# Where the second matmul's slots stand around the units of the first, in a convolution and two-layer kernel on one core

## Chip, cores and metric

One core of a Trainium2 chip. The metric is the device time of one execution in microseconds; the kernel before took 684.85 us in the median of five runs (684.1 to 686.18).

## The reference

`x` has the shape (8, 4096, 192), in float32. Each of 8 heads of 24 channels is convolved causally along the sequence with 7 taps, which are the softmax of the head's row of `weight`. The result, taken as 32768 rows of 192, goes through two matrices with a leaky ReLU between them.

```python
w = softmax(weight)                                   # (8, 7)
y[b, s, h*24+g] = sum_k w[h, k] * x_pad[b, s+k, h*24+g]   # 6 zero rows ahead
h = y.reshape(32768, 192) @ w_in                      # (192, 2048)
out = np.maximum(0.01 * h, h) @ w_out                 # (2048, 192)
```

## The kernel before

**Tiles.** Channels lie on partitions. Two batches are worked on at a time: partitions 0 to 63 hold 64 channels of the one (`e = 0`), 64 to 127 those of the other (`e = 1`), and the 192 channels are three such chunks (`NCH`). A block is 512 positions of such a pair of batches, and there are 32 blocks. The first three are cut in halves of 256: `groups` 0 to 5 are half blocks, group 6 on are full blocks.

**The way of a block.** GpSimd's queue loads x and casts it to bf16 (`load_x`, L83). SyncE's queue transposes it by DMA (`transpose_x`, L98). VectorE convolves it, seven instructions for each chunk (`conv_jobs`, L205 and L211), into `yt`. TensorE multiplies by `w_in` in units (`mm1`, L466) into one of two PSUM tiles `ph`, and ScalarE evacuates each with the leaky ReLU into `g` (L473). TensorE multiplies `g` by `w_out` in slots, and the result is evacuated and stored by SyncE's queue.

**Units and slots.** A unit of `mm1` yields 128 x 1024 values of g: 24 matmuls make two units of a half block, 12 of 512 columns two of a full block (in groups up to 6; behind that, tiles of 64*64 double the number). A unit needs one of the two `ph` tiles, so it waits for the activation of the unit before the last. Up to group 6 the second matmul is done by `mm2_row_slot`: one slot is two matmuls of 192 columns (L492), one on each half of TensorE's rows, for one pair of output tiles of 128 rows. Sixteen slots are a round; between the two rounds of a pair the halves change places, and an instruction of ScalarE, the seal (L527, later the evacuation L603), keeps the second round behind the first. After a pair's second round its first tile is evacuated, at the next seal the second, and then the store is issued (L609). From group 7 on `mm2_slot` does the second matmul with the operands exchanged (L555), and VectorE evacuates with a transpose (L577).

**The order.** It is written out by hand (the schedule is manual): each engine does its instructions in program order. A group is cut into steps, four for a half block and eight for a full one. A step is two units, and then a number of slots that `plan` gives, which belong to g of earlier groups:

```python
    plan = {
        0: [0] * 4,
        NSW - 2: [16, 8, 8, 16],
        NSW - 1: [8, 8, 16, 16],
        NSW: [16, 8, 8, 16, 8, 8, 16, 16],
    }
```

`NSW` is 6. Groups 1 to 3 have 16 slots in each step, and later groups a number for each of eight steps. Loads (`load_x`) and transposes (`transpose_x`) of later blocks are issued at fixed steps, after the slots. In half blocks VectorE's jobs for the next group come after the slots too.

**The start.** The first half block does not wait for the usual way: SyncE loads it in float32 (L125), it is cast (L138), and TensorE transposes it (`transpose_first`, L157 for the first half block with `q == 0`, L166 for two others) into PSUM tiles `ptr`, one of 128 positions each for `q == 0`. ScalarE evacuates the first and VectorE the second (`evac_first`, L177), and the convolution of the first groups runs on TensorE with diagonal matrices (`pe_conv_jobs`, L236). Junk matmuls (`warm`, L332) fill TensorE's time before.

Of the kernel before, what the change touches and what calls it, by code (L numbers as in the profile page):

```python
# [10 lines left out]
FP32 = mybir.dt.float32  # L11
BF16 = mybir.dt.bfloat16
# [3 lines left out]
def kernel(  # L16
# [8 lines left out]
    nc = tc.nc  # L25
# [11 lines left out]
    NCH = D // CH  # L37
# [3 lines left out]
    HS = SUB // 2  # L41
# [63 lines left out]
    def new_xt(rp):  # L105
# [7 lines left out]
    x_half = {  # L113
        q: const_pool.tile([128, NCH, HS, 2, CH], BF16, name=f"x_half{q}") for q in (0, 3)
    }
# [27 lines left out]
    ptr = {}  # L143

    def transpose_first(q):
        n = HS if q == 0 else 1
        ts = [
            psum_o.tile(
                [128, HS // n, NCH, 128], BF16 if q else FP32, name=f"ptr{i}", tag="po"
            )  # L150
            for i in range(n)
        ]
        for s in range(HS):
            t = ts[s * n // HS]
            for c in range(NCH):
                if q == 0:
                    nc.tensor.matmul(  # L157
                        out=t[:, 0, c, :],
                        lhsT=x_half[q][:, c, s, :, :].rearrange("p e k -> p (e k)"),
                        rhs=ident,  # L160
                        start=True,
                        stop=True,
                    )
                    continue
                for e in range(2):
                    nc.tensor.transpose(  # L166
                        out=t[e * CH : (e + 1) * CH, s, c, :],
                        in_=x_rows[q][:, e, s, c * CH : (c + 1) * CH],
                        identity=ident,
                    )  # L170
        ptr[q] = [t[:, s] for t in ts for s in range(HS // n)]
# [104 lines left out]
    for sign, off in ((1, 0), (-1, GRP - 1)):  # L276
        nc.gpsimd.affine_select(
            out=sel, in_=sel, compare_op=mybir.AluOpType.is_ge, fill=0.0,
# [31 lines left out]
    ident = const_pool.tile([128, 128], BF16)  # L310
# [3 lines left out]
    for rows in (0, 128):  # L314
# [6 lines left out]
        out=w_out.rearrange("p (c i) d -> p c i d", i=RUN),  # L321
        in_=moe_w_out.rearrange("(c p i) d -> p c i d", p=128, i=RUN),
# [123 lines left out]
    NSW = 2 * NHALF  # L446
# [7 lines left out]
    def mm1(grp, u, M):  # L454
        blk, t0, T = grp
        y = yt[blk]
        nf = ST // T
        ph = psum_h.tile([128, 2, ST], FP32, name="ph", tag="ph")
        chunks = range(NCH) if blk or t0 else FIRST
        for n in range(nf * NCH):  # L460
            i, c = n // NCH, chunks[n % NCH]
            f = nf * u + i
            for e in range(2):
                ps = slice(e * CH, (e + 1) * CH)
                for m in range(0, 128, M):
                    nc.tensor.matmul(  # L466
                        out=ph[m : m + M, e, i * T : (i + 1) * T],
                        lhsT=w_in_of(f, e, c, m, m + M),
                        rhs=y[ps, c, t0 : t0 + T],
                        start=(c == chunks[0]),  # L470
                        stop=(c == chunks[-1]),
                    )
        act = nc.scalar.activation(  # L473
            out=g[blk][:, nf * u : nf * (u + 1), :, t0 : t0 + T],
            in_=ph.rearrange("p e (i t) -> p i e t", i=nf),
            func=mybir.ActivationFunctionType.Prelu, alpha=0.01,
        )
        return act
# [21 lines left out]
    def mm2_row_slot(q):  # L500

        p, fc = divmod(q, 2 * NFC)
        rnd, fc = divmod(fc, NFC)
        pair = (2 * p, 2 * p + 1)
        first, last = fc == 0, fc == NFC - 1
        if first and rnd == 0:
            for n in pair:
                po[n] = psum_o.tile([128, D], FP32, name="po", tag="po")  # L510
        for rt in range(2):
            ins = mm2_one(
                rt, pair[rt ^ rnd], fc, first and rnd == 0, last and rnd == 1
            )
            if first and rnd == 1:
                sync(ins, seal, "both row tiles have left these banks")
        if last and rnd == 0:
            seal_round(p, ins)
        if last and rnd == 1:
            evac_o(pair[0])  # L520
# [14 lines left out]
    def mm2_slot(q):  # L535

        nonlocal seal
        gi, fc = divmod(q, NR * NFC)
        rnd, fc = divmod(fc, NFC)
        first, last = fc == 0, fc == NFC - 1
        if first:
            for r in ((1, 0), (2,), ())[rnd]:
                acc2[gi, r] = psum_o.tile([128, ST], FP32, name="acc2", tag="po")
        for rt in range(2):
            r = (rnd + rt) % NR
            fresh = (rnd, rt) in ((0, 0), (0, 1), (1, 1))  # L550
            done = (rnd, rt) in ((1, 0), (2, 0), (2, 1))
            b, t0, T = groups[gi]
            ps = slice(rt * CH, (rt + 1) * CH)
            for e in range(2):
                ins = nc.tensor.matmul(  # L555
                    out=acc2[gi, r][e * CH : (e + 1) * CH, 0:T],
                    lhsT=w_out_of(ps, fc, r),
                    rhs=g[b][ps, fc, e, t0 : t0 + T],
                    start=first and fresh,
                    stop=last and done,  # L560
                )
                if first and not fresh:
                    sync(ins, seal, "the other row tile has left this bank")
        if last and rnd < 2:
            seal = nc.scalar.copy(out=junk, in_=junk)  # L565
            sync(seal, ins, "between the rounds")
        if last and rnd > 0:
            for r in ((), (1,), (0, 2))[rnd]:
                evac_t(gi, r)
# [26 lines left out]
    def evac_o(n):  # L596
# [21 lines left out]
        NSW - 1: [8, 8, 16, 16],  # L618
        NSW: [16, 8, 8, 16, 8, 8, 16, 16],
    }  # L620
    slot = 0
    for i, grp in enumerate(groups):
        blk, t0, T = grp
        steps = T // 64
        if t0 == 0:
            g[blk] = g_pool.tile([128, NFC, 2, ST], BF16, name="g", tag="g")
        quota = plan.get(i, [16] * 4 if T == HT else [5, 5, 6, 5, 5, 6, 8, 8])

        if i == 0:
            ahead = []  # L630
        else:
            ahead = conv_jobs(groups[i + 1]) if i + 1 < len(groups) else []
        per = -(-len(ahead) // steps)
        for j in range(steps):
            for u in range(2 * j, 2 * j + 2):
                mm1(grp, u, 128 if i <= NSW else CH)
                if i == 0 and u == 0:
                    conv_1 = conv_jobs(groups[1], (1,))
                    for job in conv_1[:3]:
                        job()  # L640
                    spread_down(1)
                    spread_up(1)
                    for job in conv_1[3:]:
                        job()
                    pe_0, evac_0 = pe_conv_jobs(groups[1], 0)
                    pe_2, evac_2 = pe_conv_jobs(groups[1], 2, cross=True)
                if i == 0 and u in CUTS:
                    cut = slice(*CUTS[u])
                    run(pe_0[cut], pe_2[cut])
                if i == 0 and u == 5:  # L650
                    evac_0(nc.vector.tensor_scalar_mul)
                    evac_2(nc.vector.tensor_scalar_mul, nc.vector.tensor_scalar_mul)
                if i == 0 and u == 6:
                    transpose_first(2)
            jobs = ahead[per * j : per * (j + 1)]
            if T == ST:


                jobs = ahead[len(ahead) * j // steps : len(ahead) * (j + 1) // steps]
                for job in jobs:  # L660
                    job()
                jobs = []
            for _ in range(quota[j]):
                if i <= NSW:
                    mm2_row_slot(slot)
                else:
                    mm2_slot(slot)
                slot += 1
            if i == 0 and j == 3:
                evac_first(2, nc.vector.tensor_copy, nc.vector.tensor_copy)  # L670
            if i == 2 and j == 1:
                transpose_x(2)
            for job in jobs:
                job()
            if i == 0 and j == 3:
                transpose_half(3)

            last_half = t0 + T == ST
            if i == NSW and j == steps - 1:
                evac_o(LAST - 1)  # L680
                slot = NSW * NR * NFC
            if j == steps // 4 and last_half:
                load_x(blk + 3)
            if j == steps // 2 and last_half and blk > 0:
                transpose_x(blk + 2)
# [35 lines left out]
```

## Time and profile before

| | us |
|---|---|
| median of five runs | 684.85 |
| runs | 684.1, 684.27, 684.85, 685.35, 686.18 |
| the profiled execution, its own time | 686.18 |
| its span, first to last instruction | 684.3 |
| TensorE busy with matmuls in the span | 679.4 |
| ScalarE busy | 522.1 |
| VectorE busy | 483.1 |
| GpSimd busy | 145.5 |

The page of the profile gives for each engine the time in which an instruction was under way. For TensorE that is from a matmul's start to its modelled end, and matmuls overlap each other. A row of the timeline merges instructions of one line: start, time from the first start to the last end, engine, line, operation, operands, form and number, and in brackets the idle time before it with what ended it. The list of waits counts only time in which an engine had nothing under way. The groups stand at these times in the trace: group 1 begins at about 20 us, group 4 at 52.4, group 5 at 61.9, group 6 at 71.3 and group 7 at 90.1.

### The profile page before, as it was taken

How to read it: one execution, taken by the hardware profiler on the slowest of the kernel's cores; microseconds unless marked ns; L12 is line 12 of the kernel's file. 1: busy time of each engine (PE TensorE's matmuls, PEld its weight loads, DVE VectorE, ACT ScalarE, POOL GpSimd, SP SyncE). 2: the span in 40 equal slices, each digit the busy share in tenths (PEclk: the TensorE clock that was granted, in tenths of full speed). 3: DMA queues.
4: the chain of work that ended last, by engine and by line, in shares of the span. 5: the costliest groups of instructions: out<-in, count | busy, mean ns of one | idle time of the engine just before them, and what ended most of it. 6: DMA issues, size and time to landing. Idle time of an engine off the chain costs nothing.

```text
span 684.3 us, 27253 instructions
## 1 busy us (share of the span) xinstructions
PE 679.4 (99%) x12514; PEld 457.6 (67%) x12514; DVE 483.1 (71%) x827; ACT 522.1 (76%) x617; POOL 145.5 (21%) x204
## 2 busy tenths in 40 slices
PE   9999999999999999999999999999999999999998
PEld 6999766666666666666666666666666666666667
DVE  6979667667687667786667786676876676876612
ACT  6889987777877778777787777777777778777781
POOL 7722250222102222012222022222022220000000
PEclk9999999999999999999999999999999999999999
DMA  9966794579566577586676576596675684333123
GB/s 154 92 88 79 98 98 60 66 70 94 79 87 78 57 79 92 75 90 74 57 89 85 81 85 71 59 94 83 82 79 64 72 94 72 71 54 35 35 48 93
DMA packets 212786, 53.27 MB, mean 78 GB/s; under 512 B 207168, under 2 KB 212288, under 8 KB 212672
## 3 DMA queue, kind: packets, MB, share of 16 engines
q1 hardware_dynamic: 113920, 37.57, 33.5%
q0 software_dynamic: 98736, 13.97, 29.9%
q8 instruction: 97, 1.59, 0.9%
q14 instruction: 17, 0.14, 0.1%
q10 hardware_dynamic: 16, 0.00, 0.0%
HBM read 28.31 MB, written 25.17 MB: 78 GB/s over the span
## 4 chain that ended last, share of the span: by engine, by line
PE 97%; ACT 2%; DMA 0%; DVE 0%; issue 0%; SPq 0%
PE ph L466 48%; PE acc L555 42%; PE po L492 6%; ACT g L473 2%; PE acc L236 1%; DMA x_nat<-in_x_dram 0%; PE ptr L157 0%; DVE xt L177 0%; PE ptr L166 0%; SPq L125 0%; ACT x_half L138 0%; DVE o_sb L603 0%
## 5 line engine op out<-in xcount | busy, mean ns | idle before, releaser
L473 ACT ACTIVATE g<-ph 128x1024 bf16<-128x1024 f32 x512 | 496.3, 1021 | 138.5 <-PE ph L466 137.9
L211 DVE SCALAR_TENSOR_TENSOR yt<-xt,wk,yt 128x512 bf16<-128x512 bf16 (+1 forms) x600 | 380.9, 713 | 0.2
L466 PE MATMUL ph<-yt,w_in 64*64 64x512 bf16 (+2 forms) x6048 | 377.6, 366 | 0.5 <-ACT g L473 0.2
L555 PE MATMUL acc<-g,w_out 64*64 64x512 bf16 x5376 | 328.2, 376 | 0.0
L466 PEld LDWEIGHTS <-w_in 64*64 64x64 bf16 (+1 forms) x6048 | 234.4, 130 | 101.3 <-issue 2.5
L555 PEld LDWEIGHTS <-w_out 64*64 64x64 bf16 x5376 | 172.4, 118 | 114.6
L83 POOL DMA_DIRECT2D x_bf<-in_x_dram x180 | 133.8, 776 | 416.0 <-DMA xt<-x_bf 294.3
L577 DVE STREAM_TRANSPOSE o_t<-acc 128x512 f32<-128x512 f32 x84 | 70.6, 884 | 175.5 <-PE acc L555 175.5
L492 PE MATMUL po<-w_out,g 64*128 64x192 bf16 (+1 forms) x896 | 48.0, 243 | 0.0
L492 PEld LDWEIGHTS <-g 64*128 64x128 bf16 (+1 forms) x896 | 44.5, 95 | 1.6 <-issue 0.4
L205 DVE TENSOR_SCALAR yt<-xt,wk 128x512 bf16<-128x512 bf16 (+1 forms) x100 | 28.1, 343 | 10.3 <-DMA xt<-x_bf 10.3
L565 ACT COPY junk<-junk 128x1 f32<-128x1 f32 x56 | 10.7, 191 | 4.3 <-ACT g L473 0.3
L603 ACT COPY o_sb<-po 128x192 f32<-128x192 f32 x24 | 7.6, 320 | 0.8
L603 DVE COPY o_sb<-po 128x192 f32<-128x192 f32 x8 | 2.8, 357 | 6.8 <-PE po L492 6.8
L236 PE MATMUL acc<-xt,diag 64*64 64x256 bf16 x140 | 7.0, 328 | 0.2 <-DVE xt L177 0.2
L236 PEld LDWEIGHTS <-diag 64*64 64x64 bf16 x140 | 5.3, 131 | 2.1 <-DVE xt L177 0.8
L332 PE MATMUL warm<-const-bfloat16-1.0 128*128 128x512 bf16 (+1 forms) x12 | 4.2, 490 | 0.8 <-PEq L705 0.8
L132 POOL DMA_DIRECT2D x_half<-in_x_dram x6 | 4.3, 764 | 0.0
L396 ACT ACTIVATE diag<-ident,whm 128x64 bf16<-128x64 bf16 x14 | 3.6, 336 | 0.2 <-DVE whm L382 0.2
L332 PEld LDWEIGHTS <-const-bfloat16-1.0 128*128 128x128 bf16 x12 | 1.4, 131 | 2.5 <-issue 2.5
L128 POOL DMA_DIRECT2D x_rows<-in_x_dram x4 | 2.9, 742 | 0.0
L424 ACT ACTIVATE yt<-acc,rsum 128x256 bf16<-128x256 f32 (+1 forms) x3 | 1.4, 473 | 1.6 <-PE acc L236 1.6
(46 smaller groups left out, 24.2 us busy)
## 6 DMA issues: line engine op xcount, KB each, us to landing
out_dram<-o_t SPq DMA_DIRECT2D x112, 192.0 KB, 3.9
x_bf<-in_x_dram POOLq DMA_DIRECT2D x180, 64.0 KB, 3.1
out_dram<-o_sb SPq DMA_DIRECT2D x12, 192.0 KB, 2.6
xt<-x_bf SPq DMA_TRANSPOSE x90, 3.3
w_out<-in_moe_w_out_dram POOLq DMA_DIRECT2D x1, 768.0 KB, 9.1
out_dram<-o_sb SPq DMA_DIRECT2D x8, 96.0 KB, 1.7
w_in<-in_moe_w_in_dram POOLq DMA_DIRECT2D x2, 256.0 KB, 4.7
x_nat<-in_x_dram SPq DMA_DIRECT2D x2, 192.0 KB, 2.9
```

The costliest lines, as they stand in the source:

```text
L83: nc.gpsimd.dma_start(out=t[:, c, :, e, :], in_=src[2 * rp + e, :, :, c * CH : (c + 1) * CH],)
L205: lambda s=src, d=dst, c=c: nc.vector.tensor_scalar_mul(d, s, wk[:, c, 0:1])
L211: lambda s=src, d=dst, c=c, k=k: nc.vector.scalar_tensor_tensor(out=d, in0=s, scalar=wk[:, c, k : k + 1], in1=d, op0=mybir.AluOpType.mult, ...
L236: lambda k=k, p=p, a=a, ps=ps, to=to, acc=accs[e * apart]: nc.tensor.matmul(out=acc[to, :T], lhsT=diag[c][ps, p, k, :], rhs=xt[0][ps, c, a ...
L332: nc.tensor.matmul(out=wa[:, 0, 0:cols], lhsT=ones[:, 0:128], rhs=ones[:, 0:cols], start=True, stop=True,)
L466: nc.tensor.matmul(out=ph[m : m + M, e, i * T : (i + 1) * T], lhsT=w_in_of(f, e, c, m, m + M), rhs=y[ps, c, t0 : t0 + T], start=(c == chun ...
L473: act = nc.scalar.activation(out=g[blk][:, nf * u : nf * (u + 1), :, t0 : t0 + T], in_=ph.rearrange("p e (i t) -> p i e t", i=nf), func=my ...
L492: return nc.tensor.matmul(out=po[m], lhsT=g[b][ps, fc, e, s * 128 : (s + 1) * 128], rhs=w_out[ps, fc, :], start=start, stop=stop,)
L555: ins = nc.tensor.matmul(out=acc2[gi, r][e * CH : (e + 1) * CH, 0:T], lhsT=w_out_of(ps, fc, r), rhs=g[b][ps, fc, e, t0 : t0 + T], start=fi ...
L565: seal = nc.scalar.copy(out=junk, in_=junk)
L577: nc.vector.transpose(out=osb[gi, 0][:, 0 : T // GB, :, r], in_=acc2.pop((gi, r))[:, 0:T].rearrange("p (j k) -> p j k", k=GB),)
L603: ins = copy(out=o_sb[:, n % 2, :], in_=po.pop(n))
```

## The change

In group 1's first step three of the 16 slots stand before the first unit, five between the two units and eight behind them. In groups 4, 5 and 6, which hold pairs of steps of eight slots, four slots of the second step of such a pair, and four of the step behind it, stand between that step's two units; the rest stands behind. The number of slots in each step is the same as before. The three transposes of the second 128 positions in `transpose_first(0)` are no longer matmuls with the identity into a float32 tile, but TensorE transposes into a bf16 tile.

```diff
@@ transpose_first
-                [128, HS // n, NCH, 128], BF16 if q else FP32, name=f"ptr{i}", tag="po"
+                [128, HS // n, NCH, 128], BF16 if q or i else FP32, name=f"ptr{i}", tag="po"
...
                 if q == 0:
-                    nc.tensor.matmul(
-                        out=t[:, 0, c, :],
-                        lhsT=x_half[q][:, c, s, :, :].rearrange("p e k -> p (e k)"),
-                        rhs=ident,
-                        start=True,
-                        stop=True,
-                    )
+                    rows = x_half[q][:, c, s, :, :].rearrange("p e k -> p (e k)")
+                    if s == 0:
+                        nc.tensor.matmul(
+                            out=t[:, 0, c, :], lhsT=rows, rhs=ident, start=True, stop=True
+                        )
+                    else:
+                        nc.tensor.transpose(out=t[:, 0, c, :], in_=rows, identity=ident)
                     continue
@@ the main loop
+    between = {(1, 0): (3, 5)}
+    for i, js in ((NSW - 2, (2, 3)), (NSW - 1, (1, 2)), (NSW, (2, 3, 5, 6))):
+        between.update({(i, j): (0, 4) for j in js})
     slot = 0
+
+    def mm2_slots(i, n):
+        nonlocal slot
+        for _ in range(n):
+            if i <= NSW:
+                mm2_row_slot(slot)
+            else:
+                mm2_slot(slot)
+            slot += 1
+
...
         for j in range(steps):
+            early = between.get((i, j), (0, 0))
             for u in range(2 * j, 2 * j + 2):
+                mm2_slots(i, early[u % 2])
                 mm1(grp, u, 128 if i <= NSW else CH)
...
-            for _ in range(quota[j]):
-                if i <= NSW:
-                    mm2_row_slot(slot)
-                else:
-                    mm2_slot(slot)
-                slot += 1
+            mm2_slots(i, quota[j] - sum(early))
```

## Prediction

> **What bounds the kernel now.** I read the page first, then the waits of TensorE, then the timeline of TensorE and of ScalarE where the diff acts. The page says that matmuls are under way nearly all the time and that the chain which ends last is almost only TensorE:
>
> ```profile
> PE 679.4 (99%) x12514; PEld 457.6 (67%) x12514; DVE 483.1 (71%) x827; ACT 522.1 (76%) x617; POOL 145.5 (21%) x204
> ...
> PE 97%; ACT 2%; DMA 0%; DVE 0%; issue 0%; SPq 0%
> ...
> L177 DVE COPY xt<-ptr x4: 346/352/358, 11.9 to 19.7; 128x384 bf16<-128x384 bf16 x4
> ...
> L177 DVE CAST xt<-ptr x1: 558/558/558, 5.8 to 5.8; 128x384 bf16<-128x384 f32 x1
> ```
>
> So only what shortens TensorE's own stream counts. The list of waits gives TensorE 0.2 us behind ScalarE (L466 behind L473) and nothing more after the start-up. That number misleads: a matmul drains for about 0.2 us after its last issue, so a stall shorter than the drain leaves no idle time. The 2% of ScalarE in the chain says that stalls exist. They are read from the distance between the starts of blocks in TensorE's timeline:
>
> ```profile
> 17.41 1.50 PE L466 MATMUL ph<-yt,w_in 64*128 64x256 bf16 x24
> 18.85 0.53 PE L166 MATMUL ptr<-ident,x_rows 128*64 128x128 bf16 x12
> 19.38 1.76 PE L466 MATMUL ph<-yt,w_in 64*128 64x256 bf16 x24
> 21.34 0.85 PE L466 MATMUL ph<-yt,w_in 64*128 64x256 bf16 x12 [0.20 <-ACT g L473]
> 21.99 1.52 PE L492 MATMUL po<-w_out,g 64*128 64x192 bf16 x32
> ...
> 54.87 1.51 PE L466 MATMUL ph<-yt,w_in 64*128 64x256 bf16 x24
> 56.18 0.86 PE L492 MATMUL po<-w_out,g 64*128 64x192 bf16 x16
> 56.84 1.76 PE L466 MATMUL ph<-yt,w_in 64*128 64x256 bf16 x24
> 58.40 0.86 PE L492 MATMUL po<-w_out,g 64*128 64x192 bf16 x16
> 59.06 1.18 PE L466 MATMUL ph<-yt,w_in 64*128 64x256 bf16 x18
> ...
> 75.06 0.86 PE L492 MATMUL po<-w_out,g 64*128 64x192 bf16 x16
> 75.72 1.76 PE L466 MATMUL ph<-yt,w_in 64*128 64x512 bf16 x12
> 77.28 0.86 PE L492 MATMUL po<-w_out,g 64*128 64x192 bf16 x16
> ```
>
> Two units of mm1 (24 matmuls of 256 columns, or 12 of 512) take 56.18 - 54.87 = 1.31 us where nothing stalls, so a unit takes 0.655; 16 matmuls of mm2 (eight slots) take 56.84 - 56.18 = 0.66 us, 0.0825 a slot. The second eight-slot step of the pair takes 58.40 - 56.84 = 1.56 for its two units: 0.25 us of stall. In the full group the same place takes 77.28 - 75.72 = 1.56 against 1.29 in the chain of waits: 0.27. The first step of the second group: the last unit of group 0 and the first of group 1 start at 19.38 and the next unit at 21.34, 1.96 instead of 1.31: 0.65 us, part before each of the two units.
>
> ScalarE's timeline says why:
>
> ```profile
> 55.11 0.32 ACT L603 COPY o_sb<-po 128x192 f32<-128x192 f32 x1
> 55.76 3.91 ACT L473 ACTIVATE g<-ph 128x1024 bf16<-128x1024 f32 x4 [0.34 <-PE ph L466]
> 59.56 0.32 ACT L603 COPY o_sb<-po 128x192 f32<-128x192 f32 x1
> ```
>
> An activation takes 1.02 us (page, L473), and back to back they start 0.92 apart (two take 1.94). mm1 has two PSUM tiles ph, so a unit needs the activation of the unit before the last to be over. Call the units of the pair A, B (first step) and C, D. ScalarE does A from 55.76, B from 56.68 to 57.70. C needs A, gone at 56.78: no wait at 56.84. D could start at 56.84 + 0.655 = 57.49, but B's tile is free only at 57.70 plus the signal: the stall of 0.25. TensorE needs 2 x 1.31 + 2 x 0.66 = 3.94 us for the pair and ScalarE 4 x 0.92 + 0.32 + small change = 4.1: nearly level, so two units side by side are too dense and the eight slots behind them come too late to help.
>
> **The change part by part.**
>
> Slots in between, eight places. Four slots move ahead of the second unit: of D, and of F, the second unit of the step behind the pair. Nothing is added; 4 x 0.0825 = 0.33 us of mm2 stands where TensorE stalled. D's turn comes at 57.49 + 0.33 = 57.82, after 57.75: stall gone. Next late: E comes after D (to 58.48) and the four slots left, 58.81; it needs C's activation, which ran 57.73 to 58.75: 0.06 us of room. F: E ends at 59.46, plus its four slots 59.79; D's activation began 58.65 and ended 59.67: 0.12 of room. Without the second between-move F would stand at 59.46 and stall 0.2; that is what the move in the step behind the pair is for. G, two units later, stands behind 12 slots (0.99 us), where ScalarE, which idles 0.34 before such a unit today, has caught up. Gain 0.25 in group 4, 0.25 in group 5, 2 x 0.27 in group 6: 1.04 us.
>
> Second group's first step. ScalarE is busy with the activations of group 0 in a row from 18.30. The first unit of group 1 is held to about 20.29, the second to 21.34 (its tile's activation started 20.26 and took 1.02). Three slots (0.25) go where the first unit waits 0.26: it starts at 20.29 as before. It ends at 20.94; five slots, 0.41, to 21.36: 0.02 past the wait. Eight slots fewer stand behind it: 8 x 0.0825 = 0.66, less 0.02: gain 0.64 us. These slots read g of the first units (activations over before 17), the PSUM tiles that pe_conv's accumulators left (evacuated by VectorE from 17.6 to 19.1) and w_out (GpSimd's queue stops waiting for its landing at 16.85): all there at 20.03.
>
> The same moves past the queues. The evacuations (L603) and the seals (L527) hang on the last slot of a round; in every step that one stays behind the second unit, so ScalarE's order is the same, and so is the order of the stores and transposes on SyncE and of the loads on GpSimd: each is issued after the same slot as before, only 0.6 to 1.9 us earlier. Behind a seal waits the first slot of the next round; in group 1 that seal runs at about 23.2 and the slot comes at 23.97, in the others two units (1.31 us) lie between. VectorE's convolution is paced by the transposes that SyncE issues behind the stores, so it moves along: for group 7 it ends at 87.6 today and its units start at 90.1; the transposes before it (69.57) come 0.64 + 0.5 earlier and the units 1.7 earlier, so 2.5 us of room become 1.9. For group 6 (68.9 against 71.3) 2.4 become about 1.9. From 90 to 660 us TensorE has not one wait, so the gain stays to the end.
>
> The boundaries. Twenty more changes between mm1 and mm2: two for each of the eight places and four in group 1. The trace of before has no switch as often as this, but it has the switch: around 56.18 and 56.84 the blocks start exactly at the pitch inside a block, cost 0. The nearest row that says otherwise is the change between 64*64 and 64*128 tiles at the start (last start of line 236 at 17.21, pitch 0.1, next block at 17.41), about 0.1 us. Both mm1 and mm2 here are 64*128. Bounds 0 and 0.1 each[...]. I take 0.
>
> The first transpose (line 157). Three of six identity matmuls become transposes that write bf16, and VectorE evacuates their tile. VectorE's cast from fp32 took 558 ns, its copies from bf16 352 ns: 0.21 us less, and the chain of waits goes through this cast (0.57 at 5.82, then TensorE's convolution at 6.44; the diagonal that it also needs is ready at 5.69). What is late next: ScalarE's cast of the other tile, over at 6.01. The transposes of line 166 (219 ns) are no dearer than the identity matmuls (314). What of 0.21 reaches the end depends on the clock. The page of the profile prints a clock of 1.00 throughout, but the pitch shows a slow start (windows of line 236, four or two tiles at a time):
>
> ```profile
> 6.50:9.50 3.00, 3.00 (x50) 2.43 (x54) 1.00 1.20 177
> 10.00:11.00 1.00, 1.00 (x32) 0.98 (x22) 1.00 1.47 179
> ```
>
> Steps of the convolution start 0.21 us apart up to about 9.85 and 0.108 after. [...] Then the 9.85 stays, one slow step more is done before it, and 0.11 us is gained. [...] I take 0.15. [...]
>
> **Sum.** 1.04 + 0.64 + 0.15 = 1.83 us. The profiled execution took 686.18 us, of which 684.3 is the span; it is the slowest of the five, 1.33 over the median. I apply the difference, not the absolute: span 682.5, median 684.85 - 1.83 = 683.0.
>
> **The rivals.**
>
> Stalls come back behind the pair. ScalarE needs 4.1 us for what TensorE does in 3.94, and E and F have only 0.06 and 0.12 us of room. If a signal or an evacuation takes 0.1 more than I booked, 0.13 per pair is lost again, 0.5 in all: 684.85 - 1.3 = 683.5. For it: the thin room. Against: ScalarE's idle 0.34 us before the first unit of each step after.
>
> [...]
>
> The boundaries cost. If each of the twenty costs what the change of tile shape costs, and weight loads no longer run ahead in blocks of eight matmuls, 20 x 0.16 = 3.2 us against 1.83: slower, 686.2. It decides from 0.09 a boundary on. Against: the boundaries present today cost nothing that the starts show.
>
> **How the numbers follow.** A measurement of this kernel can tell about 0.2%, 1.37 us, from no change. My forecast 0.66 (faster by over that; its own range 682.3 to 683.7, from the two values of the start-up and the spread of single runs). The stalls returned 0.16 and the late clock 0.10 both end within 0.2%; together 0.26. Boundaries 0.08, slower. The range leaves out the slower case and little beyond: 682.2 (all of 0.21, and half a microsecond of spread) to 684.7 (the late clock).
>
> **What would show it.** TensorE's starts: units of the pair and its four slots in a row at 0.655 and 0.33, no 1.56 anywhere; first slot at 20.0, the second unit of group 1 near 21.2, group 7 at 88.2 to 88.3 instead of 90.1; ScalarE's share of the chain near 0; the cast of 558 ns gone, a fifth copy of about 352; the quick pitch near 9.7 to 9.9. Wrong if: the units E or F show a gap; a block of four slots lasts over 0.35; the slow pitch goes on to 13; or TensorE waits for VectorE at 70 or 88.

## The result and the profile after

The changed kernel took 682.6 us in the median of 22 runs against 684.46 of the kernel before (43 runs): 1.86 us less. The ratio is 0.9975, with a 95% interval of 0.9968 to 0.9981, so it is faster, by a quarter of a per cent. Forecast were 683.0 us and a gain of 1.83. The gain is the number to compare: the 684.85 us from which the 683.0 was counted was the median of five runs, and that of all 43 lies 0.39 lower.

The profiled executions differ by more, 684.3 against 680.8 us of span, and that is not the change alone. Runs of both kernels lie on two levels about 1.6 us apart (before 684.1 to 684.9 and 685.3 on; after 682.1 to 683.0 and 684.0 on). In the traces the level goes with the moment at which TensorE's quick pitch begins, that is, at which the steps of the convolution start 0.11 us apart instead of 0.21. In the five traces of runs on the upper level (before is one of them, from 9.85 us on) that moment lies 3.4 to 4.0 us behind the convolution's first matmul; in the eight others (after is one) the pitch is quick from that matmul on. The same 84 matmuls of the convolution, before and after:

```profile
6.44 4.92 PE L236 MATMUL acc<-xt,diag 64*64 64x256 bf16 x84 [0.23 <-DVE xt L177]
5.90 3.46 PE L236 MATMUL acc<-xt,diag 64*64 64x256 bf16 x84 [0.23 <-ACT diag L396]
```

What the change itself does is therefore read from stretches of the trace behind the start.

The page of the changed kernel, TensorE's list of waits and the groups on the tile `ptr`:

```profile
PE 676.5 (99%) x12514; PEld 450.4 (66%) x12514; DVE 482.0 (71%) x827; ACT 521.6 (77%) x617; POOL 145.9 (21%) x204
...
PE 99%; ACT 0%; DVE 0%; issue 0%
...
PE warm L332 <- PEq L715: 0.8, 1, 0.8
PE acc L236 <- ACT diag L396: 0.2, 1, 0.2
...
L177 DVE COPY xt<-ptr x5: 348/357/358, 5.5 to 17.9; 128x384 bf16<-128x384 bf16 x5
L163 PE MATMUL ptr<-ident,x_half x3: 298/311/311, 4.9 to 5.2; 128*128 128x128 bf16 x3
```

ScalarE has left the chain (2% before), and TensorE waits for no activation any more. The fp32 cast of 558 ns has become a fifth copy of about 357 ns, and the transposes (311 ns, L163) last no longer than the identity matmuls before (314). TensorE's timeline at the places of the change (start, time from first start to last end):

```profile
17.02 0.53 PE L166 MATMUL ptr<-ident,x_rows 128*64 128x128 bf16 x12
17.55 0.85 PE L466 MATMUL ph<-yt,w_in 64*128 64x256 bf16 x12
18.21 0.44 PE L492 MATMUL po<-w_out,g 64*128 64x192 bf16 x6
18.47 0.85 PE L466 MATMUL ph<-yt,w_in 64*128 64x256 bf16 x12
19.12 0.61 PE L492 MATMUL po<-w_out,g 64*128 64x192 bf16 x10
19.53 0.85 PE L466 MATMUL ph<-yt,w_in 64*128 64x256 bf16 x12
20.19 0.85 PE L492 MATMUL po<-w_out,g 64*128 64x192 bf16 x16
...
53.72 0.86 PE L492 MATMUL po<-w_out,g 64*128 64x192 bf16 x16
54.38 0.85 PE L466 MATMUL ph<-yt,w_in 64*128 64x256 bf16 x12
55.03 0.53 PE L492 MATMUL po<-w_out,g 64*128 64x192 bf16 x8
55.36 0.85 PE L466 MATMUL ph<-yt,w_in 64*128 64x256 bf16 x12
56.02 0.53 PE L492 MATMUL po<-w_out,g 64*128 64x192 bf16 x8
56.35 0.85 PE L466 MATMUL ph<-yt,w_in 64*128 64x256 bf16 x12
57.00 0.53 PE L492 MATMUL po<-w_out,g 64*128 64x192 bf16 x8
57.33 0.85 PE L466 MATMUL ph<-yt,w_in 64*128 64x256 bf16 x12
57.99 1.19 PE L492 MATMUL po<-w_out,g 64*128 64x192 bf16 x24
...
86.58 1.52 PE L466 MATMUL ph<-yt,w_in 64*64 64x512 bf16 x24
```

Read the starts: units follow each other in steps of 0.655 plus their slots (54.38 to 55.03, 0.65; 55.03 to 55.36, 0.33), and nowhere is there the 1.56 of before. The start of group 0's last unit (17.55, 19.38 before) and the start of group 7 (86.58, 90.09 before) enclose all the slots that moved: 69.03 us against 70.71, 1.68 us less, which is the 0.64 + 1.04 of the prediction. Before, group 7 begins with

```profile
90.09 1.52 PE L466 MATMUL ph<-yt,w_in 64*64 64x512 bf16 x24
```

From group 7 to the end of the span both need 594.2 us.

ScalarE's timeline, group 4:

```profile
52.64 0.32 ACT L603 COPY o_sb<-po 128x192 f32<-128x192 f32 x1
53.30 3.98 ACT L473 ACTIVATE g<-ph 128x1024 bf16<-128x1024 f32 x4 [0.34 <-PE ph L466]
57.17 0.31 ACT L603 COPY o_sb<-po 128x192 f32<-128x192 f32 x1
57.37 1.96 ACT L473 ACTIVATE g<-ph 128x1024 bf16<-128x1024 f32 x2
59.21 0.33 ACT L603 COPY o_sb<-po 128x192 f32<-128x192 f32 x1
59.87 3.98 ACT L473 ACTIVATE g<-ph 128x1024 bf16<-128x1024 f32 x4 [0.32 <-PE ph L466]
```

From 53.30 on ScalarE works nearly in a row until 59.54, then idles 0.32 us: it is behind for one pair and the step after, and has caught up at the next, as forecast.

### The profile page after: what moved, and what is told of

The parts are those of the page before. It is cut to its first block, busy times and chain, and to the rows that moved or that the text cites. A ratio compares the mean times of both kernels' runs of the same rounds, so it can differ in the third digit from the quotient of the medians.

```text
span 680.8 us, 27253 instructions
## 1 busy us (share of the span) xinstructions
PE 676.5 (99%) x12514; PEld 450.4 (66%) x12514; DVE 482.0 (71%) x827; ACT 521.6 (77%) x617; POOL 145.9 (21%) x204
## 4 chain that ended last, share of the span: by engine, by line
PE 99%; ACT 0%; DVE 0%; issue 0%
PE ph L466 49%; PE acc L555 43%; PE po L492 6%; PE acc L236 1%; PE warm L332 1%; PE ptr L166 0%; ACT xt L177 0%; DVE o_sb L603 0%; PE ptr L159 0%; PE wps L368 0%; ACT diag L396 0%; PE warm L368 0%
## 5 line engine op out<-in xcount | busy, mean ns | idle before, releaser
L466 PEld LDWEIGHTS <-w_in 64*64 64x64 bf16 (+1 forms) x6048 | 231.3, 130 | 102.2 <-issue 0.8
L555 PEld LDWEIGHTS <-w_out 64*64 64x64 bf16 x5376 | 169.1, 118 | 117.9
L492 PE MATMUL po<-w_out,g 64*128 64x192 bf16 (+1 forms) x896 | 49.8, 243 | 0.0
L565 ACT COPY junk<-junk 128x1 f32<-128x1 f32 x56 | 10.7, 191 | 4.3 <-ACT g L473 0.4
L236 PE MATMUL acc<-xt,diag 64*64 64x256 bf16 x140 | 5.6, 272 | 0.2 <-ACT diag L396 0.2
```

The source lines that it names most:

```text
L236: lambda k=k, p=p, a=a, ps=ps, to=to, acc=accs[e * apart]: nc.tensor.matmul(out=acc[to, :T], lhsT=diag[c][ps, p, k, :], rhs=xt[0][ps, c, a ...
L466: nc.tensor.matmul(out=ph[m : m + M, e, i * T : (i + 1) * T], lhsT=w_in_of(f, e, c, m, m + M), rhs=y[ps, c, t0 : t0 + T], start=(c == chun ...
L492: return nc.tensor.matmul(out=po[m], lhsT=g[b][ps, fc, e, s * 128 : (s + 1) * 128], rhs=w_out[ps, fc, :], start=start, stop=stop,)
L555: ins = nc.tensor.matmul(out=acc2[gi, r][e * CH : (e + 1) * CH, 0:T], lhsT=w_out_of(ps, fc, r), rhs=g[b][ps, fc, e, t0 : t0 + T], start=fi ...
```

## The experiments

The theory is that the stalls were won, 0.64 us in group 1 and 1.04 in the pairs, and 0.1 to 0.2 by the evacuation. The rivals are the start-up and its clock, stalls that come back, and boundaries that cost. "The stretch" is from the start of group 0's last unit to the start of group 7. Medians are compared with those of the kernel before that were taken beside them, 684.48 to 684.50. The diffs are against the changed kernel where nothing else is said.

**Slots alone**

```diff
-                [128, HS // n, NCH, 128], BF16 if q or i else FP32, name=f"ptr{i}", tag="po"
+                [128, HS // n, NCH, 128], BF16 if q else FP32, name=f"ptr{i}", tag="po"
...
-                    if s == 0:
+                    if s >= 0:
```

> The change without its transposes: all six of the first transposes are identity matmuls into float32 again, the slots stand as in the changed kernel. Stall theory: the stalls of TensorE are what was won, 0.64 in group 1 and 1.04 in the pairs, so 1.68 us faster than before (about 682.8). Rival (the start-up and its clock did it, since the two profiled spans differ by 3.5 us and 1.8 of that lies ahead of 20 us): less than half of that, 0.3 to 0.8 us.

682.88 us, 1.61 faster than before (ratio 0.9978, 0.9970 to 0.9985); the stretch is 69.03 us, as with the whole change.

**Transposes alone**

```diff
-    between = {(1, 0): (3, 5)}
-    for i, js in ((NSW - 2, (2, 3)), (NSW - 1, (1, 2)), (NSW, (2, 3, 5, 6))):
-        between.update({(i, j): (0, 4) for j in js})
+    between = {}
```

> The transposes alone, slots as before. Stall theory: 0.1 to 0.2 us faster than before (684.3), all four stalls of the pairs and those of group 1 in the trace as before. Rival (start-up and clock): 1 to 1.8 us faster. [...]

684.32 us, 0.17 less by the medians; the ratio of 1.0003 (0.9992 to 1.0015) can't tell that from nothing. The stretch is 70.70. The other way to the same term, the whole change against the slots alone, gives 682.88 - 682.60 = 0.28. So the term is small, and its size can't be read from medians; the rival of the start-up, which asked for over 1 us, is out. The traces bound it: where the quick pitch is late, the convolution starts at 5.92 us with the transposes and at 6.12 without (first step alone, pairs alone), 0.20 earlier; where it is early, at 5.90 (whole change) and 5.99 (slots alone), 0.09 earlier.

**Group 1's first step alone, and the pairs alone** (both without the transposes)

```diff
 # first:
-    for i, js in ((NSW - 2, (2, 3)), (NSW - 1, (1, 2)), (NSW, (2, 3, 5, 6))):
-        between.update({(i, j): (0, 4) for j in js})
 # second:
-    between = {(1, 0): (3, 5)}
+    between = {}
```

> Only group 1's first step is laid out anew (3, 5, 8 slots); pairs and transposes as before. Stall theory: 0.64 us faster; the time from group 0's last unit to the start of group 7 is 70.71 - 0.64 = 70.07 us in the trace. Rival (a gain in group 1 is given back later, since transposes, stores or VectorE don't move along): under 0.3.

> Only the eight places (0, 4) in groups 4 to 6; group 1's first step and the transposes as before. Stall theory: 1.04 us faster; the time from group 0's last unit to the start of group 7 is 70.71 - 1.04 = 69.67 us. Rival (ScalarE, with 4.1 us of work for 3.94 of TensorE, makes the stall come back two units later): 0.5 us faster, and gaps before the units behind the pair.

683.81 us (0.68 less; ratio 0.9992, 0.9983 to 1.0002) and 683.42 (1.07 less; 0.9991, 0.9983 to 1.0000). The two levels of the runs make these intervals wide, and the times alone can't tell either part from nothing. The stretches can. First step alone, then pairs alone:

```profile
19.16 0.85 PE L466 MATMUL ph<-yt,w_in 64*128 64x256 bf16 x12
89.22 1.52 PE L466 MATMUL ph<-yt,w_in 64*64 64x512 bf16 x24
...
19.33 1.76 PE L466 MATMUL ph<-yt,w_in 64*128 64x256 bf16 x24
89.00 1.52 PE L466 MATMUL ph<-yt,w_in 64*64 64x512 bf16 x24
```

They are 70.07 and 69.67 us, that is 0.64 and 1.04 less than 70.71, and the sum is the 1.68 of both. Nothing is given back later: from group 7's first matmul to TensorE's last, all of these traces, before and after too, need 590.80 us.

**Only the pair's second step**

```diff
-    for i, js in ((NSW - 2, (2, 3)), (NSW - 1, (1, 2)), (NSW, (2, 3, 5, 6))):
+    for i, js in ((NSW - 2, (2,)), (NSW - 1, (1,)), (NSW, (2, 5))):
```

> The changed kernel with the between-slots of the step behind each pair taken back; those of the pair's second step stay (four places (0, 4) instead of eight). Stall theory: unit F, the second of the step behind, then stands 0.33 us too early and waits 0.2 to 0.29 us, so 0.8 to 1.1 us of the 1.04 are lost: the stall has moved by two units; 683.3 to 683.7. Rival (the first of the two moves is enough): 682.6 as the changed kernel.

683.92 us (ratio 0.9992, 0.9979 to 1.0005), and the stretch is 70.33, 1.30 longer than with the whole change and 0.26 longer than with no slot between in the pairs at all. Half of the edit is worse than none. TensorE's timeline, and the row of ScalarE's whose fourth activation is D's:

```profile
55.44 0.85 PE L466 MATMUL ph<-yt,w_in 64*128 64x256 bf16 x12
56.10 0.53 PE L492 MATMUL po<-w_out,g 64*128 64x192 bf16 x8
56.43 1.83 PE L466 MATMUL ph<-yt,w_in 64*128 64x256 bf16 x24
58.06 1.52 PE L492 MATMUL po<-w_out,g 64*128 64x192 bf16 x32
...
53.37 3.98 ACT L473 ACTIVATE g<-ph 128x1024 bf16<-128x1024 f32 x4 [0.34 <-PE ph L466]
```

D (55.44) has no wait. The two units behind it take 58.06 - 56.43 = 1.63 instead of 1.31: F, which starts at 57.40, now stalls by 0.32 behind D's activation, over at 53.37 + 3.98 = 57.35. The stall has moved by two units and grown. TensorE's list of waits for this kernel shows none of it: 0.2 us of it lie under the drain of the matmuls before, and a gap of the 0.13 left is not listed (the shortest in these lists are 0.2).

**Two slots between instead of four**

```diff
-        between.update({(i, j): (0, 4) for j in js})
+        between.update({(i, j): (0, 2) for j in js})
```

> The changed kernel with two instead of four slots between in all eight places. Stall theory, counted in slots: four slots (0.33 us) overfill a stall of 0.25 to 0.27, two (0.165) leave 0.09 to 0.1 of it in the pair's second step, and the step behind, which two slots must also cover, has 0.1 to 0.2 left: 0.4 to 1.2 us slower than the changed kernel (683.0 to 683.8), with gaps before the second units that are 0.165 us longer than without. Rival (any slot in between is enough, since it is the order and not the amount that counts): 682.6.

682.87 us (ratio 0.9976, 0.9965 to 0.9987); the stretch is 69.41, 0.38 longer than with four, 0.095 for each of the four pairs. That is just short of the 0.4 to 1.2 expected, because the step behind lost nothing.

```profile
54.30 0.85 PE L466 MATMUL ph<-yt,w_in 64*128 64x256 bf16 x12
54.95 0.36 PE L492 MATMUL po<-w_out,g 64*128 64x192 bf16 x4
55.20 0.85 PE L466 MATMUL ph<-yt,w_in 64*128 64x256 bf16 x12
55.85 0.69 PE L492 MATMUL po<-w_out,g 64*128 64x192 bf16 x12
56.35 0.85 PE L466 MATMUL ph<-yt,w_in 64*128 64x256 bf16 x12
57.01 0.36 PE L492 MATMUL po<-w_out,g 64*128 64x192 bf16 x4
57.17 0.85 PE L466 MATMUL ph<-yt,w_in 64*128 64x256 bf16 x12
```

Two slots are 0.165 us, but 55.20 - 54.95 is 0.25: 0.09 of the stall is left in the pair's second step. In the step behind, 57.17 - 57.01 = 0.16: none. So it is the amount of work in between that counts, and for the pair's second step the count of the stall agrees to 0.01 us.

**More boundaries**

```diff
+    for i in (1, 2, 3):
+        between.update({(i, j): (0, 8) for j in range(4) if (i, j) != (1, 0)})
```

> The changed kernel, and in the other eleven steps of groups 1 to 3, where nothing stalls, 8 of the 16 slots stand between the two units as well: 22 more boundaries between mm1 and mm2 in tiles of 64*128. No cost of a boundary: the same time, 682.6, and 69.03 us from group 0's last unit to group 7. Rival (a boundary costs about 0.1 us, as the change of tile shape at the start does): 2.2 us slower, 684.8.

683.88 us (ratio 0.9994, 0.9985 to 1.0002), the stretch 70.04: 1.01 longer. That looked like the rival, at half its price, but the loss sits in six places only. Timeline of TensorE at two of them, and the row of the list of waits (all engines) that the changed kernel does not have:

```profile
22.14 0.85 PE L466 MATMUL ph<-yt,w_in 64*128 64x256 bf16 x12
22.87 0.83 PE L492 MATMUL po<-w_out,g 64*128 64x192 bf16 x16
...
26.17 0.82 PE L466 MATMUL ph<-yt,w_in 64*128 64x256 bf16 x12
26.83 0.82 PE L492 MATMUL po<-w_out,g 64*128 64x192 bf16 x16
27.49 0.82 PE L466 MATMUL ph<-yt,w_in 64*128 64x256 bf16 x12
28.32 0.83 PE L492 MATMUL po<-w_out,g 64*128 64x192 bf16 x16
...
PEld L492 <- ACT o_sb L603: 1.4, 5, 0.3
```

27.49 to 28.32 is 0.83 us for a unit of 0.655. The slots that come next open a second round and need the seal, an evacuation of ScalarE that stands behind the activation of the unit before; with one unit instead of two ahead of them they come too early. Five rounds at 0.19 us by the starts, and the first (22.14 to 22.87, the seal of L527) at 0.08, make the 1.01 to within 0.03. To tell it from the boundaries, those steps were left alone (the diff is against the kernel with more boundaries):

```diff
-        between.update({(i, j): (0, 8) for j in range(4) if (i, j) != (1, 0)})
+        between.update({(i, j): (0, 8) for j in (0, 2) if (i, j) != (1, 0)})
```

> The changed kernel, with 8 of the 16 slots between the units only in those further steps of groups 1 to 3 whose slots open a pair of output tiles (five steps, 10 more boundaries); the steps whose slots open a second round, which waits for a seal, stay as they are. If a boundary is free and what the run with all eleven steps lost was the seal: the same time as the changed kernel and 69.03 us from group 0's last unit to group 7. Rival (boundaries cost): 10/22 of the 1.01 us that were lost there, 0.46 us.

The stretch is 69.03 us, the same to the hundredth with ten more boundaries. (Median 682.8, ratio 0.9977, 0.9966 to 0.9987.) And from group 7 on, in tiles of 64*64:

```diff
-            early = between.get((i, j), (0, 0))
+            early = between.get((i, j), (0, 2) if i > NSW else (0, 0))
```

> The changed kernel, and from group 7 on two of each step's slots stand between the two units: 224 places, 448 more boundaries, in tiles of 64*64. No cost of a boundary: the same time within 0.3 us. Rival: 0.01 us a boundary would already show as 4.5 us, 0.1 as 45 us. A seal between rounds now stands ahead of a unit's activation in some steps; if that delays ScalarE, single gaps of up to 0.3 us before a unit.

682.83 us (ratio 0.9979, 0.9970 to 0.9988). From group 7 to the end 594.44 us against 594.25 (to TensorE's last matmul 590.99 against 590.80): 0.19 us for 448 boundaries, of which 0.15 lie in a single gap at 550.2 us, where the weights of the next slot wait for a seal (L565). A boundary between mm1 and mm2 in the same tile shape cost nothing that these starts show.

**All six transposes**

```diff
-                [128, HS // n, NCH, 128], BF16 if q or i else FP32, name=f"ptr{i}", tag="po"
+                [128, HS // n, NCH, 128], BF16, name=f"ptr{i}", tag="po"
...
-                    if s == 0:
+                    if s < 0:
```

> The changed kernel with the other three identity matmuls as bf16 transposes too, so that ScalarE also evacuates from bf16. If VectorE's evacuation ends the wait and the clock does not care: the same as the changed kernel within 0.15 us. [...]

682.63 us (ratio 0.9967, 0.9959 to 0.9976; the medians of this and the changed kernel are 0.03 apart). 4 of its 20 runs lie on the upper level and a fifth (683.45) between the two, against 6 of 22 of the changed kernel and 17 of 47 of the kernel before (11 of 48 in another set of its runs). So the median does not rise, and no more of the executions start late; counts as small as these could still hide a modest rise.

**Group 0 in tiles of 64*64**

```diff
-                mm1(grp, u, 128 if i <= NSW else CH)
+                mm1(grp, u, 128 if 0 < i <= NSW else CH)
```

> The changed kernel with group 0's units in tiles of 64*64, as the convolution on TensorE between them has, so that the six changes of tile shape in group 0 go (starts 0.20 us apart there instead of 0.1). If a change of shape costs 0.09 to 0.1 us: 0.3 to 0.5 us faster than the changed kernel, 682.2, less what ScalarE, which is busy in a row from the sixth unit on, takes back. Rival (twice as many matmuls and weight loads make the units longer than 0.655 us): the same or slower.

684.63 us (ratio 1.0003, 0.9995 to 1.0011), 2 us slower than the changed kernel, against the forecast. The changes of shape in group 0 are gone (at five of their six places the next start now comes within 0.04 us, 0.20 in the changed kernel), but TensorE stands still twice:

```profile
11.52 1.29 PE L466 MATMUL ph<-yt,w_in 64*64 64x256 bf16 x29
13.72 0.77 PE L466 MATMUL ph<-yt,w_in 64*64 64x256 bf16 x19 [0.92 <-issue]
...
17.61 0.24 PE L166 MATMUL ptr<-ident,x_rows 128*64 128x128 bf16 x1
18.83 0.50 PE L166 MATMUL ptr<-ident,x_rows 128*64 128x128 bf16 x11 [0.97 <-DMA x_bf<-in_x_dram]
```

The first stands in the middle of a unit (11.52, then 13.72), with "issue": nothing that the profile shows was waited for; weights wait there too. For the second the view names a load of `x_bf`, which these transposes do not read (they read `x_rows`). Starts before and after are 1.18 and 1.21 us apart. In the trace packets of the instruction queue (16 KB) begin at 11.45 and 16.55, about a microsecond each, and end 0.1 us ahead of both. The author's guess, that TensorE had run out of instructions, since this kernel issues twice as many in group 0, was not shown: the changed kernel has such packets too (11.46 and 17.14) and no standstill, and no run tests it. The cause stays open.

## Why the prediction was right

**The stalls**: hidden in a busy TensorE, read from starts. 0.64 in group 1 (70.71 to 70.07) and 1.04 in the pairs (70.71 to 69.67) are the booked terms to 0.01 us, shown by each part alone. The reason given for the hiding was only nearly right: stalls of 0.25 are longer than the drain of 0.2, and the rest is a gap too short for the list.

**Late next**: E and F did not stall, and the move in the step behind the pair is needed. But the room was misread. The time that counts runs from the end of D's issue: 0.20 drain, 0.04 until the activation begins, 1.02 activation, 0.05 signal, 1.31 in all (with half of the edit D is issued by 56.09 and F starts at 57.40). One unit and eight slots are 0.655 + 0.66 = 1.315. In the changed kernel exactly that lies between the end of C and the start of E, and between D and F, so the room was about 0.01 us for each, not 0.06 and 0.12. The booking left out the signal behind the activation and took D's activation from the trace of before (over at 59.67), though D starts 0.07 later with four slots ahead of it. That the sum came out just above nothing and not just below is luck. With half of the edit one unit and four slots lie there, 0.985, and 0.32 is missing; "stall 0.2" for F was 0.32 in the group that the timeline shows and 0.33 by 1.30/4 on average.

**The start-up**: booked 0.15 between 0.11 and 0.21. The medians (0.17 in one pair of kernels, 0.28 in the other) can't tell such a term from nothing; by the traces the convolution starts 0.20 earlier where the quick pitch is late and 0.09 where it is early. So the size is right, as far as can be told. The forecast of the pitch was not: "near 9.7 to 9.9" is close for executions on the upper level (5.92 + 3.63 = 9.55 with the transposes alone, 6.12 + 4.04 = 10.16 with the pairs alone), while the profiled one of the changed kernel has it from the convolution's first matmul on, and so all its places (first slot at 18.2, group 7 at 86.6) lie 1.6 to 1.8 us ahead of those forecast. That the 9.85 stays was an assumption that these traces do not bear out. Nor did the quick pitch come a fixed time after TensorE's restart: late starts of it came 3.42 (before, more boundaries), 3.63 (transposes alone, first step alone), 4.04 (pairs alone) us after the convolution's first matmul, and in the eight other traces it was there from that matmul on. What sets the moment, no run here shows.

**The rivals**: stalls returned, out (no gap in the trace of after), by the 0.01 us above; the late clock (a quick pitch that begins later), out as a shift of the median (six transposes, 682.63 us against 682.60); boundaries, out (69.03 with ten more; 0.19 us for 448; the 0.16 us each of the forecast was not shown).

**The sum**: 1.68 in the stretch and 0.09 to 0.20 ahead of it make 1.77 to 1.88; measured 1.86, by medians that can't tell 0.1 us.

## What to carry to other kernels

With two PSUM tiles, a unit can start only when the unit before the last is drained, activated and signalled: here 1.31 us after the end of its issue, and 0.27 more where it stood right behind another unit, since the activations are then 0.92 apart and the units 0.655. Count how much of TensorE's work lies between (one unit and the slots: 0.655 + 8 x 0.0825 = 1.315 just suffices for units that stand apart; neighbours need 1.58, which is twelve slots), and spread the filler by that count through the following step too; stopping after the first stall only moved it, and made it larger. Keep slots that wait for another engine (the seal) behind two units while doing so.

## What the runs showed of the hardware

Stalls of TensorE of 0.25 to 0.33 us in these traces appeared neither as idle time nor in the list of waits; they were seen in the distance between the starts. Changing between two streams of matmuls of the same tile shape cost nothing that the starts show (0.19 us for 448 changes), also in blocks of four matmuls (0.16 us for two slots in the step behind), while a change between 64x128 and 64x64 tiles took about 0.1 us (starts 0.20 apart against 0.11). Not expected: executions whose quick pitch began late were about 1.6 us longer, nearly as much as this change is worth, and twice the instructions in a short stretch came with two standstills of 1.2 us, of open cause.
